# Gate logits as a 97th FFN column, the last 96 FFN columns unpacked, and VectorE steps split in halves, in a planned attention + SwiGLU kernel

## The chip, the cores and the metric

The kernel runs on one core of one Trainium2 chip. The metric is device microseconds of one execution; a kernel's time is the median of its runs.

## The reference

One activation x of 2048 tokens by 512 features (bf16) goes through two branches, which a gate mixes per token:

```python
g = sigmoid((x * gate_w).sum(-1, keepdims=True))
# branch a: 32 heads of 16, causal sliding window of 256 tokens
qkv = (x @ wqkv)                      # 512 -> 3 * 512
scores = q @ k.T * 16 ** -0.5         # kept where 0 <= query - key < 256
a = softmax(scores) @ v @ wo
# branch b: SwiGLU with F = 1376
b = (silu(x @ w1) * (x @ w3)) @ w2
out = g * a + (1 - g) * b
```

## The kernel before

**Tiling.** Tokens are cut into four tiles t of 512 (and sixteen m of 128). Heads come in four groups c of eight. F = 1376 is ten chunks f of 128 columns and a last one of 96 (`NFC` = 11, `FL` = 96). x stands transposed in SBUF (`xT`), the first half by TensorE transposes, the second by DMA transposes.

**Attention.** `add_proj` computes Q and K of one (c, t): four matmuls of 128 x 512 into one PSUM bank, then a copy to SBUF. K is copied twice, once with the odd and once with the even heads set to zero, by the factors in `maskEO`; `evac_k` (L336) does this in one VectorE instruction of 1024 elements per partition. A *burst* (`add_burst`, L636) computes the scores of up to 512 query columns for four head pairs, into the four banks of the PSUM tile `big`; ScalarE takes one exponential over them (L644); GpSimd cuts the window's edges (L660), and for some edges VectorE does (L654). There are 76 bursts, 4 or 5 for each (c, t). `add_pv` (L710) multiplies by V and by ones (for the denominators) into two banks; `turn` (L720) transposes each bank into SBUF, `norm` (L729, L730) divides both halves in two instructions, `back` (L735) transposes into `OT`, and `add_out` (L589, L596) multiplies by wo, mixes and stores.

**FFN.** `add_up` (L460) computes w1 and w3 of one (t, f) into a bank each. With silu(v) = v/2 (1 + tanh(v/2)), ScalarE takes the tanh (L436), VectorE multiplies twice (L441, L468) into `hT`. The last 96 columns are handled by `add_up_last` for two token tiles at once: they are cut into pieces of 32 columns, four pieces stand side by side in the array's columns, and three units of 16 small matmuls (L510) take the place of four units of four. `add_down` (L559) multiplies by w2 in 11 matmuls, and the result is scaled by (1 - g)/2 from `omg` (L565 on ScalarE, L568 on VectorE).

**Gate.** gate_w is broadcast to 128 partitions early by a GpSimd DMA (L163). `add_z` (L403): 16 VectorE multiplies with a running sum give the logits `zt`. The first half reads the x tiles that the transposes used, the second half a copy of x loaded anew, 1 MB, into a part of `OT` that is still free (L166). `add_gate`: a small tanh (L414) and two small VectorE steps (L417, L419) give `gq` and `omg`.

**What sets the order.** Everything after the first loads is an `Op` with its engine, an assumed duration, what it depends on, and which buffers it takes and frees: four PSUM banks `g`, the tile `big`, nine exponential buffers and others. A planner places ops by assumed times, one by one, and writes each engine's instruction order, which the engines then follow with semaphores. Bursts have due times 2.66 us apart. Where a burst isn't due, other work fills TensorE: projections, V, FFN units in a fixed sequence. Two rules matter here. While at most one bank is free (`tight`), ScalarE and VectorE prefer work that frees a bank; this rule stands in both kernels. And a first matmul of an FFN pair (`o.gate`) steps back while a tanh waits on ScalarE:

```python
elif o.kind == "ffn":
    k = 2 if backlog < 1 or not o.gate else 3.5
```

Of the kernel before, what the change touches and what calls it, by code (L numbers as in the profile page):

```python
# [22 lines left out]
def kernel(  # L23
# [37 lines left out]
    w1_sb = pp.tile([P, NDC, F], BF16, name="w1_sb")  # L61
# [4 lines left out]
    maskEO = pp.tile([P, 1, 2, 1], F32, name="maskEO")  # L66
    scr = pp.tile([P, 2], F32, name="scr")
    zt = pp.tile([P, NT], F32, name="zt")
# [3 lines left out]
    smpool = ctx.enter_context(tc.tile_pool(name="sm", bufs=3))  # L72
    ps = ctx.enter_context(tc.tile_pool(name="ps", bufs=1, space=bass.MemoryType.PSUM))

    class Op:
        def __init__(self, engs, dur, fn, deps=(), acq=(), rel=(), rank=0.0, need=None, kind="", lag=0.0):
            self.engs = engs if isinstance(engs, tuple) else (engs,)
            self.dur, self.fn, self.rank, self.kind, self.lag = dur, fn, rank, kind, lag
            self.deps = [d for d in deps if d is not None]
            self.acq, self.rel, self.need = acq, rel, need  # L80
            self.start = self.end = self.eng = None
            self.users = []
            self.gate = False
            self.cont, self.head, self.tiled = False, self, False
            ops.append(self)
# [21 lines left out]
    def x_dma(t, h):  # L107
        if t == 0:
            xs = xp.tile([P, 2, D], BF16, name=f"xs{h}")[:]
        else:  # L110
            if h == 0:
                xs_tiles["pair"] = xp.tile([P, 4, D], BF16, name="xs23")
            xs = xs_tiles["pair"][:, 2 * h:2 * h + 2, :]
        nc.sync.dma_start(
            out=xs,
            in_=x2d[512 * t + 256 * h:512 * t + 256 * (h + 1), :].rearrange("(m p) d -> p m d", p=P))
        xs_tiles[2 * t + h] = xs
# [41 lines left out]
    gw = OT[:, S:S + D]  # L159
    xn = OT[:, 2 * S:4 * S].rearrange("p (m d) -> p m d", d=D)  # L160

    def gate_dma():
        nc.gpsimd.dma_start(out=gw, in_=gate_w.rearrange("(x d) -> x d", x=1).to_broadcast([P, D]))  # L163

    def xn_dma():
        nc.sync.dma_start(out=xn, in_=x2d[S // 2:S, :].rearrange("(m p) d -> p m d", p=P))  # L166
# [7 lines left out]
    land["wo"], land["xn"], land["gate"] = 40.0, 40.0, 10.0  # L174
# [9 lines left out]
    nc.vector.tensor_reduce(out=maskEO[:, 0, 0, :], in_=eo[:], axis=mybir.AxisListType.X, op=ALU.add)  # L184
    nc.vector.tensor_scalar(out=maskEO[:, 0, 1, :], in0=maskEO[:, 0, 0, :], scalar1=-1.0, scalar2=1.0,
# [14 lines left out]
    gate_dma()  # L200
# [100 lines left out]
    def add_proj(c, t0, t1, is_q):  # L301
# [4 lines left out]
        hold("g", key, 1)  # L306
# [25 lines left out]
        def evac_k(eng):  # L332
            kt = qk_tile[(c, t)][0][:, 2 * o0:2 * (o0 + n)].rearrange("p (j i b) -> p j i b", i=2, b=HK)
            src = g_tile[key][:, 0:n].rearrange("p (j x b) -> p j x b", x=1, b=HK)
            sh = [P, n // HK, 2, HK]
            nc.vector.tensor_tensor(out=kt, in0=src.to_broadcast(sh), in1=maskEO[:].to_broadcast(sh),  # L336
                                    op=ALU.mult)
# [12 lines left out]
        else:  # L350
            bs = [Op("DVE", 1.16 * n / 512 + 0.05, evac_k, [a], rel=[("g", key)], rank=-0.5)]
# [45 lines left out]
    z_op, gate_op = [], {}  # L397

    def add_z(m):

        def f(eng):
            x = xs_tiles[m // 2][:, m % 2, :] if m < NT // 2 else xn[:, m - NT // 2, :]
            nc.vector.scalar_tensor_tensor(out=x, in0=x, scalar=1.0, in1=gw, op0=ALU.mult,  # L403
                                           op1=ALU.mult, accum_out=zt[:, m:m + 1])

        deps = xT_op[m // 2] if m < NT // 2 else [loads["xn"]]
        z_op.append(Op("DVE", 0.7, f, deps + [loads["gate"]], rank=1.5))

    def add_gate(t):

        ms = slice(4 * t, 4 * t + 4)

        def th(eng):
            nc.scalar.activation(out=zt[:, ms], in_=zt[:, ms], func=ACT.Tanh, scale=0.5)  # L414

        def fin(eng):
            nc.vector.tensor_scalar(out=gq[:, ms], in0=zt[:, ms], scalar1=0.5,  # L417
                                    scalar2=0.5, op0=ALU.mult, op1=ALU.add)
            nc.vector.tensor_scalar(out=omg[:, ms], in0=zt[:, ms], scalar1=-0.25,  # L419
                                    scalar2=0.25, op0=ALU.mult, op1=ALU.add)  # L420

        d = Op("ACT", 0.25, th, z_op[4 * t:4 * t + 4], rank=1.0)
        gate_op[t] = Op("DVE", 0.35, fin, [d], rank=1.0)
# [3 lines left out]
    def h_of(t):  # L427
        if t not in h_tile:
            h_tile[t] = sb.tile([P, NFC, 512], BF16, name=f"hT{slot('hT', t)}")
        return h_tile[t]  # L430

    def half_swish(tl, key, kt_, kh, m):

        def th(eng):
            tl["tt"] = sb.tile([P, 512], BF16, name=f"tt{slot('tt', kt_)}")
            nc.scalar.activation(out=tl["tt"][0:m, :], in_=g_tile[key][0:m, :], func=ACT.Tanh,  # L436
                                 scale=0.5)

        def s1(eng):
            tl["h1"] = sb.tile([P, 512], BF16, name=f"h1_{slot('h1', kh)}")  # L440
            nc.vector.scalar_tensor_tensor(out=tl["h1"][0:m, :], in0=tl["tt"][0:m, :], scalar=1.0,  # L441
                                           in1=g_tile[key][0:m, :], op0=ALU.add, op1=ALU.mult)
        return th, s1

    first_h = {}

    def add_up(t, f):

        kg, ku, kt_, kh = ("G", t, f), ("U", t, f), ("tt", t, f), ("h1", t, f)
# [3 lines left out]
        hold("h1", kh, 1)  # L453
        tl = {}

        def pe(key, wsb, d0):
            def fn():
                b = bank(key) if d0 == 0 else g_tile[key]
                for dc in range(d0, d0 + 1):
                    nc.tensor.matmul(b[:], lhsT=wsb[:, dc, f * P:(f + 1) * P],  # L460
# [4 lines left out]
        th, s1 = half_swish(tl, kg, kt_, kh, P)  # L465

        def s2(eng):
            nc.vector.tensor_tensor(out=h_of(t)[:, f, :], in0=tl["h1"][:], in1=g_tile[ku][:],  # L468
                                    op=ALU.mult)
# [3 lines left out]
        a0, a = pe_unit(0.87, [pe(kg, w1_sb, i) for i in range(NDC)], [w], acq=[("g", kg)],  # L473
# [3 lines left out]
        b = Op("ACT", 0.6, th, [a], rel=[("g", kg)], acq=[("tt", kt_)], rank=0.3, kind="tanh")  # L477
        a0.gate = True
        d = Op("DVE", 0.68, s1, [b], rel=[("g", kg), ("tt", kt_)], acq=[("h1", kh)])
        new = t not in first_h  # L480
        if new:
            hold("hT", t, 4)
        e = Op("DVE", 0.68, s2, [d, u] + ([] if new else [first_h[t]]),
               rel=[("g", ku), ("h1", kh)], acq=[("hT", t)] if new else [])
        first_h.setdefault(t, e)
        up_done.setdefault(t, []).append(e)
        return [a0, u0]

    def add_up_last(ta, tb):

        f0 = (NFC - 1) * P
        keys = [("L", ta, i) for i in range(3)]
        kt_, kh = [("tt", ta, "L", i) for i in range(2)], [("h1", ta, "L", i) for i in range(2)]
        for k, n in zip(keys, (2, 2, 3)):
            hold("g", k, n)
        for i in range(2):
            hold("tt", kt_[i], 1)
            hold("h1", kh[i], 2 - i)  # L500
        tiles = [[(w1_sb, 0, ta), (w1_sb, 1, ta), (w1_sb, 2, ta), (w1_sb, 2, tb)],
                 [(w3_sb, 0, ta), (w3_sb, 1, ta), (w3_sb, 2, ta), (w3_sb, 2, tb)],
                 [(w1_sb, 0, tb), (w1_sb, 1, tb), (w3_sb, 0, tb), (w3_sb, 1, tb)]]
        assert FL == 96

        def pe(i, dc):
            def fn():
                b = bank(keys[i]) if dc == 0 else g_tile[keys[i]]
                for u, (w, p, t) in enumerate(tiles[i]):
                    nc.tensor.matmul(b[32 * u:32 * u + 32, :],  # L510
                                     lhsT=w[:, dc, f0 + 32 * p:f0 + 32 * p + 32],
                                     rhs=xT[:, dc, 512 * t:512 * (t + 1)],
                                     start=(dc == 0), stop=(dc == NDC - 1), skip_group_check=True)
            return fn

        def prod(eng, t, lo, hi, h1, key, h0, u0):
            n = hi - lo
            nc.vector.tensor_tensor(out=h_of(t)[lo:hi, NFC - 1, :], in0=h1["h1"][h0:h0 + n, :],
                                    in1=g_tile[key][u0:u0 + n, :], op=ALU.mult)

        x = [a + b for a, b in zip(xdep(512 * ta, 512 * ta + 512), xdep(512 * tb, 512 * tb + 512))]
        units = [pe_unit(0.9, [pe(i, dc) for dc in range(NDC)], [loads["wb"]], acq=[("g", keys[i])],
                         kind="ffn", more=x) for i in range(3)]
        for a0, _ in units:
            a0.tiled = True
        tls = [{}, {}]
        sw = [half_swish(tls[0], keys[0], kt_[0], kh[0], P),
              half_swish(tls[1], keys[2], kt_[1], kh[1], 64)]
# [468 lines left out]
```

## Time and profile before

| | us |
|---|---|
| median of 3 runs | 234.25 (234.06 to 234.43) |
| the profiled execution | 234.06 |
| its span, first to last instruction | 232.3 |
| TensorE busy | 222.7 |
| VectorE, ScalarE, GpSimd busy | 181.1, 176.6, 173.7 |
| start of the first and of the last burst | 12.9, 213.2 |

Times inside the profile count from the span's start. DVE is VectorE, ACT ScalarE, POOL GpSimd, SP the engine that issues most DMAs, PE TensorE's matmuls and PEld its weight loads, which overlap them. Busy shares are means over the span; where an engine waited, the profile names what ended the wait.

### The profile page before, as it was taken

To read this page: it belongs to the slowest core of one execution; us is meant where nothing else is said; L and a number is where in the kernel's file an instruction comes from. 1 tells how busy PE (TensorE), PEld (TensorE's weight loads), DVE (VectorE), ACT (ScalarE), POOL (GpSimd) and SP (SyncE) were. 2 spreads that over 40 slices of the span, in tenths; PEclk is the share of its full clock that TensorE was granted. 3 is DMA by queue.
4 is the path that set the end of the run, shared out by engine and by line. 5 is a ranking of instruction groups with operands and counts; after the bars stand their busy time and mean duration, and the time that the engine had idled before them with its cause. 6 is when DMAs were issued, how large, how long until landed. Compare 5 with 4: busy or idle time off the path is not lost.

```text
span 232.3 us, 7327 instructions
## 1 busy us (share of the span) xinstructions
PE 222.7 (96%) x3073; PEld 102.7 (44%) x3107; DVE 181.1 (78%) x321; ACT 176.6 (76%) x147; POOL 173.7 (75%) x395
## 2 busy tenths in 40 slices
PE   7999999999999999999999999999999999999992
PEld 3644344435344444435353535444444444454441
DVE  1698798999999895977867894959887977867544
ACT  2589987789887889787988898878788876877220
POOL 8059888899989888868778877778687867767500
PEclk9999999999999999999999999999999999999999
DMA  6999990020200000000000000000000020100202
GB/s 170 342 268 306 293 367 15 3 48 3 51 2 3 3 0 3 4 1 3 0 3 3 3 0 3 0 3 4 0 3 4 0 95 3 69 24 23 70 3 90
DMA packets 16096, 13.27 MB, mean 57 GB/s; under 512 B 6080, under 2 KB 15776, under 8 KB 16064
## 3 DMA queue, kind: packets, MB, share of 16 engines
q1 hardware_dynamic: 15104, 11.44, 16.6%
q0 software_dynamic: 432, 1.25, 2.5%
q8 instruction: 24, 0.39, 0.7%
q10 hardware_dynamic: 528, 0.13, 0.3%
q14 instruction: 8, 0.07, 0.1%
HBM read 8.55 MB, written 2.10 MB: 46 GB/s over the span
## 4 chain that ended last, share of the span: by engine, by line
PE 85%; ACT 4%; POOL 4%; issue 4%; DVE 1%; DMA 1%; DVEq 0%; POOLq 0%; ACTq 0%
PE big L636 10%; PE g_4000 L559 1%; PE g_4322 L559 1%; PE g_2777 L559 1%; PE g_2299 L559 1%; PE g_1951 L559 1%; POOL e_3211 L660 1%; POOL e_3063 L660 1%; PE g_4162 L559 1%; PE g_2058 L559 1%; PE g_4507 L559 1%; PE g_4482 L559 1%; PE g_4520 L559 1%; PE g_1328 L559 1%; PE g_2549 L559 1%
## 5 line engine op out<-in xcount | busy, mean ns | idle before, releaser
L460 PEld LDWEIGHTS <-w_sb 128*128 128x128 bf16 x320 | 28.8, 98 | 35.7 <-issue 4.7
L710 PEld LDWEIGHTS <-Vn 64*32 64x32 bf16 x736 | 15.5, 91 | 4.3 <-issue 2.3
L710 PEld LDWEIGHTS <-Vs 64*32 64x32 bf16 x736 | 15.5, 91 | 0.1
L735 DVE STREAM_TRANSPOSE OT<-on 128x512 bf16<-128x512 bf16 (+1 forms) x17 | 11.4, 671 | 0.1
L589 PEld LDWEIGHTS <-OT 128*128 128x128 bf16 x68 | 6.3, 98 | 6.9 <-issue 0.4
L321 PEld LDWEIGHTS <-wq_sb 128*128 128x128 bf16 x68 | 6.3, 98 | 6.7 <-issue 0.6
L321 PEld LDWEIGHTS <-wk_sb 128*128 128x128 bf16 x68 | 6.1, 98 | 6.5 <-issue 1.0
L368 PEld LDWEIGHTS <-xT 128*128 128x128 bf16 x64 | 5.7, 98 | 6.6 <-issue 0.4
L392 POOL DMA_DIRECT2D Vs<-Vn x4 | 2.5, 617 | 7.2 <-ACT Vn L376 7.2
L559 PEld LDWEIGHTS <-hT_3267 128*128 128x128 bf16 (+1 forms) x44 | 4.1, 97 | 4.9
L559 PEld LDWEIGHTS <-hT_1265 128*128 128x128 bf16 (+1 forms) x44 | 4.0, 98 | 4.8 <-issue 0.6
L559 PEld LDWEIGHTS <-hT_383 128*128 128x128 bf16 (+1 forms) x44 | 4.0, 98 | 4.6 <-issue 0.2
L403 DVE SCALAR_TENSOR_TENSOR OT<-OT 128x512 bf16<-128x512 bf16 x8 | 6.0, 762 | 0.0
L559 PEld LDWEIGHTS <-hT_2312 128*128 128x128 bf16 (+1 forms) x44 | 3.9, 98 | 4.7 <-issue 0.4
L660 POOL TENSOR_SCALAR_AFFINE_SELECT e_4456<-e_4456 64x256 bf16<-64x256 bf16 x8 | 3.5, 432 | 1.8 <-ACT e_4456 L644 1.4
L720 DVE STREAM_TRANSPOSE xs_4595<-g_4527 128x256 f32<-128x256 f32 x1 | 0.5, 450 | 5.2 <-PE g_4528 L710 5.2
L958 PE MATMUL g_141<-tt_87 128*128 128x512 bf16 x7 | 3.2, 630 | 1.3 <-DVE tt_87 L104 1.3
L660 POOL TENSOR_SCALAR_AFFINE_SELECT e_269<-e_269 64x256 bf16<-64x256 bf16 x6 | 3.7, 611 | 0.8 <-ACT e_269 L644 0.6
L660 POOL TENSOR_SCALAR_AFFINE_SELECT e_967<-e_967 64x256 bf16<-64x256 bf16 x6 | 3.8, 639 | 0.4
L660 POOL TENSOR_SCALAR_AFFINE_SELECT e_686<-e_686 64x256 bf16<-64x256 bf16 x6 | 3.2, 532 | 0.9 <-ACT e_686 L644 0.6
L660 POOL TENSOR_SCALAR_AFFINE_SELECT e_4280<-e_4280 64x256 bf16<-64x256 bf16 x6 | 2.8, 469 | 1.1 <-ACT e_4280 L644 0.8
L510 PEld LDWEIGHTS <-w_sb 128*32 128x32 bf16 x96 | 2.2, 96 | 2.9 <-issue 1.1
(949 smaller groups left out, 849.5 us busy)
## 6 DMA issues: line engine op xcount, KB each, us to landing
out_dram<-ot SPq DMA_DIRECT2D x15, 128.0 KB, 1.7
w_sb<-in_B_w_dram SPq DMA_DIRECT2D x2, 864.0 KB, 7.4
w_sb<-in_B_w_dram SPq DMA_DIRECT2D x1, 1280.0 KB, 7.6
Vs<-Vn POOLq DMA_DIRECT2D x8, 136.0 KB, 4.1
w_sb<-in_B_w_dram SPq DMA_DIRECT2D x2, 512.0 KB, 8.7
OT<-in_A_x_dram SPq DMA_DIRECT2D x1, 1024.0 KB, 10.4
e_89<-in_A_wqkv_dram SPq DMA_DIRECT2D x1, 512.0 KB, 5.7
xs_98<-in_A_x_dram SPq DMA_DIRECT2D x2, 256.0 KB, 5.9
```

What stands on the lines that cost most here:

```text
L321: nc.tensor.matmul(b[:, 0:n], lhsT=(wq_sb if is_q else wk_sb)[:, dc, c * P:(c + 1) * P], rhs=xT[:, dc, t0:t1], start=(dc == 0), stop=(dc = ...
L368: nc.tensor.matmul(b[:], lhsT=xT[:, c, m * P:(m + 1) * P], rhs=wv_sb[:, c, :], start=(c == 0), stop=(c == NDC - 1))
L392: nc.gpsimd.dma_start(out=Vs[0:HK, ms, 0:VW], in_=Vn[HK:P, ms, 0:VW])
L403: nc.vector.scalar_tensor_tensor(out=x, in0=x, scalar=1.0, in1=gw, op0=ALU.mult, op1=ALU.mult, accum_out=zt[:, m:m + 1])
L460: nc.tensor.matmul(b[:], lhsT=wsb[:, dc, f * P:(f + 1) * P], rhs=xT[:, dc, t * 512:(t + 1) * 512], start=(dc == 0), stop=(dc == NDC - 1))
L559: nc.tensor.matmul(b[:], lhsT=h_tile[t][0:fs, f, (m % 4) * P:(m % 4 + 1) * P], rhs=w2_sb[0:fs, f, :], start=(f == 0), stop=(f == NFC - 1))
L589: nc.tensor.matmul(b[:, 0:n], lhsT=OT[:, c * S + m * P:c * S + (m + 1) * P], rhs=wo_t[c // 2][:, c % 2, n0:n1], start=(c == 0), stop=(c == ...
L636: nc.tensor.matmul(big[:, u, col:col + q1 - q0], lhsT=kt[32 * u:32 * u + 32, (j % 8) * P:(j % 8 + 1) * P], rhs=qt[32 * u:32 * u + 32, q0 - ...
L660: nc.gpsimd.affine_select(out=tri, in_=tri, pattern=[[0, 4], [-1 if far else 1, HK]], compare_op=ALU.is_ge, fill=0.0, base=-1 if far else ...
L710: nc.tensor.matmul(pv[i][32 * u:32 * u + 32, a - qa:b - qa], lhsT=v_of(j, i, 4 * c + u), rhs=e_tile[k][i * HK:i * HK + HK, u, col:col + b ...
L735: nc.vector.transpose(out=OT[:, c * S + qa:c * S + qb], in_=st["on"][:, 0:nb].rearrange("p b i d -> p (b i d)"))
L958: nc.tensor.matmul(b[:], lhsT=warm[:, 0:P], rhs=warm[:], start=(i == 0), stop=(i == NWARM - 1))
```

## The change

- The last 96 columns of F are a chunk like the others, per token tile: four matmuls for w1 and four for w3. `add_up_last` and its packed matmuls go.
- The gate's logit is a 97th column: `w1_sb` has one column more, loaded with gate_w by a GpSimd DMA of 512 two-byte elements, issued when the eighth burst is recorded. The tanh of this chunk covers 97 rows (into float32, tile `xs2`), and its row 96 is tanh of half the logit. SP sends that row to a DRAM tile `zd` and fetches it back as 128 x 4 (`put`, `get`); two VectorE steps then make `gq` and `omg`. The 16 VectorE sums, the second load of x, the broadcast and the small tanh go.
- The last chunk stands fifth in a tile's sequence of chunks (ninth in the first tile).
- K's copy becomes two VectorE instructions of 512 elements; `norm` becomes two pairs, one for each half, which may start after the first transpose.
- The planner's rule on waiting tanhs goes. The bookkeeping that the packing needed (`first_h`, `tiled`) goes with it.

The diff, cut to its core:

```diff
-    w1_sb = pp.tile([P, NDC, F], BF16, name="w1_sb")
+    w1_sb = pp.tile([P, NDC, F + 1], BF16, name="w1_sb")
...
     def gate_dma():
-        nc.gpsimd.dma_start(out=gw, in_=gate_w.rearrange("(x d) -> x d", x=1).to_broadcast([P, D]))
-
-    def xn_dma():
-        nc.sync.dma_start(out=xn, in_=x2d[S // 2:S, :].rearrange("(m p) d -> p m d", p=P))
+        nc.gpsimd.dma_start(out=w1_sb[:, :, F:F + 1],
+                            in_=gate_w.rearrange("(c p x) -> p c x", p=P, x=1))
...
-        def evac_k(eng):
-            kt = qk_tile[(c, t)][0][:, 2 * o0:2 * (o0 + n)].rearrange("p (j i b) -> p j i b", i=2, b=HK)
-            src = g_tile[key][:, 0:n].rearrange("p (j x b) -> p j x b", x=1, b=HK)
-            sh = [P, n // HK, 2, HK]
-            nc.vector.tensor_tensor(out=kt, in0=src.to_broadcast(sh), in1=maskEO[:].to_broadcast(sh),
-                                    op=ALU.mult)
+        def evac_k(i):
+            def f(eng):
+                kt = qk_tile[(c, t)][0][:, 2 * o0:2 * (o0 + n)].rearrange(
+                    "p (j i b) -> p j i b", i=2, b=HK)[:, :, i, :]
+                src = g_tile[key][:, 0:n].rearrange("p (j b) -> p j b", b=HK)
...
+                    nc.vector.tensor_scalar_mul(out=kt, in0=src, scalar1=maskEO[:, i:i + 1])
+            return f
...
-            bs = [Op("DVE", 1.16 * n / 512 + 0.05, evac_k, [a], rel=[("g", key)], rank=-0.5)]
+            bs = [Op("DVE", d, evac_k(i), [a], rel=[("g", key)], rank=-0.5) for i in range(2)]
...
-    def add_z(m):
...
-    def add_gate(t):
...
+    def add_gate(t, b, tl, row):
...
+        def put(eng):
+            nc.sync.dma_start(out=zd[t:t + 1, :], in_=tl["tt"][row:row + 1, :])
+
+        def get(eng):
+            st["gt"] = smpool.tile([P, 4], F32, name="gt")
+            nc.sync.dma_start(out=st["gt"][:], in_=zd[t, :].rearrange("(j p) -> p j", p=P))
...
+        d = Op("SP", 3.5, put, [b])
+        e = Op("SP", 4.5, get, [d])
+        gate_op[t] = Op("DVE", 0.35, fin, [e])
...
     def add_up(t, f):
+        fs = fsz(f)
+        has_z = f == NFC - 1
...
+            m = fs + 1 if has_z and key == kg else fs
...
-                    nc.tensor.matmul(b[:], lhsT=wsb[:, dc, f * P:(f + 1) * P],
+                    nc.tensor.matmul(b[0:m, :], lhsT=wsb[:, dc, f * P:f * P + m],
                                      rhs=xT[:, dc, t * 512:(t + 1) * 512],
...
+            if has_z:
+                tl["tt"] = xp.tile([P, 512], F32, name="xs2")
+                m = fs + 1
...
-        a0.gate = True
...
-    def add_up_last(ta, tb):
...
-        def norm(eng):
-            rden = sb.tile([P, 2, 16, 1], F32, name="rden")
...
+        def norm(i):
+            def f(eng):
...
-        n1 = Op("DVE", 0.5 + nq * 0.0011, norm, [b0, b1], rank=rk)
+        n0 = Op("DVE", 0.4 + nq * 0.0007, norm(0), [b0], rank=rk)
+        n1 = Op("DVE", 0.4 + nq * 0.0007, norm(1), [b1, n0], rank=rk)
...
-        for f in range(NFC - 1):
+        zat = 4 if t else 8
+        for n, f in enumerate(list(range(zat)) + [NFC - 1] + list(range(zat, NFC - 1))):
...
-            if t % 2 == 0 and f == 10:
-                ffn += held + add_up_last(t, t + 1)
-                held = []
...
-        if t % 2 == 0 and 10 > 9:
-            ffn += add_up_last(t, t + 1)
...
-                        k = 2 if backlog < 1 or not o.gate else 3.5
+                        k = 2
...
-            if not wo_t and o in burst_ops[7:] and done.issuperset(z_op[0:4]):
+            if o is burst_ops[7]:
                 wo_dma()
-                xn_dma()
-            done.add(o)
+                gate_dma()
```

## The prediction

> **What bounds the kernel now.** I read the page's engine table first, then its slices, then the stretches, the chain of waits and the wait list.
>
> ```profile
> span 232.3 us, 7327 instructions
> ...
> PE 222.7 (96%) x3073; PEld 102.7 (44%) x3107; DVE 181.1 (78%) x321; ACT 176.6 (76%) x147; POOL 173.7 (75%) x395
> ...
> PE   7999999999999999999999999999999999999992
> ...
> PEclk9999999999999999999999999999999999999999
> ```
>
> TensorE is busy 96% of the span, in every slice but the first and the last, at a granted clock of 0.998. The others stand at 75 to 78%. A busy TensorE need not be at its peak, so I check that it does not wait. The stretches cut at the first and the last score burst:
>
> ```profile
> 0.00:12.90 12.90, 11.40 (x72) 6.56 (x73) 6.19 (x17) 5.60 (x10) 5.53 (x19) 1.00 0.86 269
> 12.90:213.20 200.30, 196.76 (x2801) 88.50 (x2835) 165.42 (x286) 167.10 (x134) 163.81 (x367) 1.00 0.16 44
> 213.20:232.30 19.10, 14.53 (x206) 7.63 (x207) 9.49 (x20) 3.94 (x4) 4.38 (x10) 0.98 0.17 57
> ```
>
> The columns after the length are PE, PEld, DVE, ACT and POOL. In the 200.3 us between the bursts TensorE lacks 3.54 us in all. The chain of waits says the same ("PE 85%", the rest in pieces), and the wait list says for what TensorE waited:
>
> ```profile
> PEld L636 <- DVE e_899 L654: 0.4, 1, 0.4
> PEld L710 <- DVE h_1_1326 L441: 0.4, 1, 0.4
> PEld L710 <- DVE hT_3267 L468: 0.4, 1, 0.4
> ...
> PEld L710 <- DVE hT_383 L468: 0.2, 1, 0.2
> ```
>
> With two of 0.2 us on the matmuls themselves (e_1713 L654, hT_2312 L468) that is 1.8 us behind VectorE, and nothing behind ScalarE or GpSimd. The rest is called issue: short gaps at changes of matmul shape. So the time is the sum of TensorE's instructions plus a start of 4.6 us and an end of about 4 us. A change counts if it lengthens that sum or makes TensorE wait.
>
> **TensorE, the term that counts.** Removed are six packed units (L510), three for each pair of token tiles. The chain prices the first three, beside a full-width unit:
>
> ```profile
> 49.36 0.86 PE g_934 L460 x4
> ...
> 60.16 0.98 PE g_1179 L510 x16
> 61.13 0.43 PE g_1199 L510 x8
> ...
> 61.89 0.55 PE g_1199 L510 x8
> 62.44 0.86 PE g_1235 L510 x16
> ```
>
> 0.98 + 0.43 + 0.55 + 0.86 = 2.82 us, and 5.64 for both triples. Added are eight full-width units (w1 and w3 for each of four tiles), at 0.86 us 6.88. The 97th weight column is free: matmuls over fewer than 128 columns or rows (the 96-row ones of L559, 0.38 us) last as long as the others. Difference **+1.24 us**. Lower bound: the second triple, by the starts in the timeline (152.16 to 153.81, 155.39 to 156.39, 156.70 to 157.03), took 2.98; 5.80 for both, or 5.96 if both cost that, so +0.92. Upper bound: had the packed groups cost exactly a quarter each, they would be 6 x 0.86 = 5.16, so +1.72. I take 1.24, from the chain.
>
> The Trainium skill (TensorEngine Tiling (Array Packing), Theoretical Speedup and Key Properties) gives a factor of up to four for at most 32 weight columns, and says that a change of tiling mode drains the array. The rows agree with the second: 0.98 against 0.86 for a packed unit that follows a full-width one. By the factor alone the sum would be 1.72 and the time 0.5 us higher.
>
> Everything else on TensorE keeps count and size. In the changed kernel's instruction order, 76 bursts stand as before; every stretch between two bursts without attention output holds at least ten full-width matmuls, eight after the four narrow bursts, as in the old order (which has packed ones among them). With a burst every 2.60 us in both kinds of stretch and an exponential of 1.88 us, a written order with a hole over 0.2 us would show a stretch with one matmul fewer. There is none, so the new order leaves TensorE no hole, if the other queues keep up.
>
> **VectorE.** Removed: 16 gate sums (L403), 11.37 us with their accumulator reads; two product steps, 46 to 44, 1.4 us. Added: each K copy (L336) in two halves. A half has 512 elements per partition from PSUM; the nearest row is Q's copy (L330), 0.68 us. 15 x (2 x 0.68 - 1.22) = 2.1; two small ones at 0.42 a half, 0.3. Normalization in halves: by the rows of the 256-wide case, 0.25 + 0.42 a half, 15 x (2 x 0.67 - 0.34 - 0.75) = 3.8. Sum: -11.4 - 1.4 + 2.4 + 3.8 = -6.6 us, 181 to about 174. It lies beside TensorE and costs nothing, since VectorE has slack; if the cover were gone, K's longer hold on its bank (1.36 against 1.22) would show as 0.1 us at each of 17 projections. ScalarE loses four small activations (0.83 us), nothing on the path.
>
> **Transfers.** Removed: the 1 MB reload of x (26.47 to 36.87 us) and the early gate broadcast on GpSimd (0.69 us of queue). No one on TensorE waited for either: zero. Added on SP, four times: one row of 2 KB out to DRAM and 512 single elements back. SP has nothing else queued then, but on VectorE the gate's two small steps wait for the return, and behind them stand the transposes that free attention output's banks. Their price is bounded by these rows (KB, us to landing):
>
> ```profile
> Vs<-Vn POOLq DMA_DIRECT2D x8, 136.0 KB, 4.1
> ...
> wk_sb<-in_A_wqkv_dram ACTq DMA_DIRECT2D x1, 128.0 KB, 3.5
> ...
> OT<-in_gate_w_dram POOLq DMA_DIRECT2D x1, 128.0 KB, 6.6
> ...
> out_dram<-ot SPq DMA_DIRECT2D x2, 64.0 KB, 1.5
> ```
>
> Out: 1.5 us. Back: between 1.5 and 6.6; I take 3.5, the row that also has 512 short pieces. A round trip is 3.0 to 8.1, likely 5.0 us. The room: for the last tile the tanh stands behind the 59th exponential, done 3.0 us after its burst (0.54 + 1.88 + 0.6), and the gate step behind K's copy in the stretch after the 62nd burst, 2.5 us after that burst. With 2.60, 2.60 and 2.10 us between those bursts the room is 7.3 - 3.0 + 2.5 = 6.8 us; the third tile has about 7.3, the others more. Likely cost zero; at the upper bound 1.3 and 0.8 us, 2.1 in all.
>
> Once, GpSimd loads the gate as a column, 512 elements of two bytes, behind the second Vs pair. In the new order that pair stands after two masks of the sixth exponential (done at 28.6 us), so the load goes out near 31 and, by 4.1 to 6.6 us, lands at 35.1 to 37.6 (38.1 with half a microsecond of delay). The 97-column matmul stands a unit and a burst after the tenth burst's start: 36.98 + 0.33 + 0.22 + 0.86 = 38.4. Zero, but closely; a load twice as slow costs up to 6 us. Neither price goes below nothing: TensorE waits for no gate transfer now.
>
> The Trainium skill (DMA: Bandwidth & Descriptors, Rules for kernel authors) says that a strided last dimension lowers to one descriptor per element, which speaks against both of these transfers. No row here shows elements that small; its fixed cost of about 2.0 us a DMA would make the round trip an estimated 4 us and the sum the same.
>
> **Sum.** The profiled execution took 234.06 us, 1.76 more than its span. 234.06 + 1.24 = 235.30. The median of the runs is 0.19 higher, 234.25, so I forecast **235.5 us**, +0.5%. A measurement of this kernel can tell about 0.2% (0.47 us) from no change.
>
> **Rivals.**
> 1. *New waits on top of the sum.* The old planner held back a first FFN matmul while a tanh was waiting; this falls away, so a bank may be taken early and freed late, and the gate adds the two waits above. For it: four banks only, and the bounds of 2.1 us (round trip) and 6 us (column). Against: the full stretches in the new order, and rows near the durations that the planner assumes. Price: 1 to 3.5 us more, 236.5 to 239.
> 2. *Not slower: relief of VectorE and GpSimd.* VectorE loses 6.6 us, most between 11 and 70 us, where it is fullest (19.7 of 20 us from 40 to 60), and there the masks on GpSimd are slowest (611 and 639 ns against 410 later). If this freed TensorE's 1.8 us of waits, the time would be 234.25 + 1.24 - 1.8 = 233.7. It decides from 0.77 us (no measurable change) and from 1.71 us (faster). Against: only 1.0 of the 1.8 us lies before 70 us (e_899, hT_383, h_1_1326), which would leave 0.24 us slower, and VectorE's work grows later.
> 3. *The packed work is cheaper to lose than it seems*, if its mode changes cost the neighbours too: the lower bound, 235.2; in the forecast's range.
>
> **How the numbers follow.** The sum alone, 234.9 to 236.2 (0.92 and 1.72 us, with some tenths of order on top): 0.72. Rival 1: 0.16. Rival 2: 0.12, of which 0.08 within 0.2% and 0.04 faster. Slower by over 0.2%: 0.72 + 0.16 = 0.88. The range leaves out rival 2 (0.12) and about half of rival 1 (0.08): 234.8 to 237.3.
>
> **What would show it.** Right: TensorE's busy time up by 1 to 1.5 us, its gap between the bursts still near 3.5 us, the last burst some 0.4 us later and the end 1.2 us later (the order has 4 matmuls more after the last burst), VectorE near 174 us. Wrong: a wait of TensorE on the gate column near 38 us, VectorE waiting for the DRAM return with TensorE idle behind it, or bursts more than 2.60 us apart because banks are held. If TensorE's missing time falls below 2 us, rival 2 is at work.

## The result and the profile after

| | before | after |
|---|---|---|
| median, us | 234.34 (234.06 to 234.59, 4 runs) | 235.80 (235.64 to 236.05, 4 runs) |
| ratio to before | | 1.0063, interval [1.0046, 1.0081] |
| profiled execution, its span | 234.06, 232.3 | 235.75, 234.1 |
| granted clock | 0.998 | 0.998 |
| start of the last burst | 213.16 | 213.56 |
| start of the last VectorE step (`ot`) | 229.01 | 230.26 |

The changed kernel is slower by 0.63%, 1.46 us between the medians; 235.5 was forecast. The page's first line, engine line and line of the chain of waits:

```profile
span 234.1 us, 7214 instructions
...
PE 223.0 (95%) x3008; PEld 103.6 (44%) x3043; DVE 177.0 (76%) x337; ACT 176.1 (75%) x144; POOL 168.3 (72%) x395
...
PE 92%; DMA 3%; issue 2%; DVE 1%; SPq 0%; DVEq 0%
```

The others have become emptier (VectorE 181.1 to 177.0, GpSimd 173.7 to 168.3), and the end is later all the same: the chain runs over TensorE for 92% of the span. The stretches, cut where the prediction cut them (PE, PEld, DVE, ACT, POOL after the length):

```profile
12.90:213.20 200.30, 196.32 (x2728) 89.72 (x2759) 160.97 (x299) 165.97 (x130) 158.91 (x367) 1.00 0.16 38
213.20:234.10 20.90, 15.65 (x210) 8.07 (x211) 11.51 (x25) 4.11 (x5) 4.52 (x11) 0.98 0.16 52
```

Between the bursts TensorE seems to lack 3.98 us, 3.54 before. The wait list gives what it waited for there:

```profile
PEld L564 <- DVE e_893 L582: 0.4, 1, 0.4
PEld L564 <- DVE h_0_661 L451: 0.4, 1, 0.4
PEld L638 <- DVE Vn L371: 0.4, 1, 0.4
PEld L638 <- DVE bsb L496: 0.2, 1, 0.2
PEld L638 <- DVE hT_1263 L457: 0.4, 1, 0.4
PEld L638 <- DVE h_0_1510 L451: 0.2, 1, 0.2
```

That is 2.0 us of idle time of weight loads with VectorE named as what ended it (1.8 before, two of those on matmuls), and none of it names the gate or its column. Kernel 4 will show that no such line is a wait of TensorE's matmuls. The timeline shows the column's matmul, the last tile's gate transfers and the end:

```profile
12.98 0.40 PE L564 MATMUL big<-qt_175,kt_174 32*128 32x320 bf16 x8
...
30.99 0.78 POOL L155 DMA_DIRECT2D w_sb<-in_gate_w_dram  x1
...
38.45 1.03 PE L434 MATMUL g_689<-xT,w_sb 128*97 128x512 bf16 x4
...
172.23 0.24 SPq L396 DMA_DIRECT2D zd<-xs_3506  x1
173.45 0.37 SPq L400 DMA_DIRECT2D gt<-zd  x1
179.23 0.37 DVE L404 TENSOR_SCALAR gq<-gt 128x4 f32<-128x4 f32 x1
...
228.93 0.38 PE L517 MATMUL g_4635<-xs_580,OT 128*128 128x256 bf16 x2
...
230.26 0.48 DVE L524 SCALAR_TENSOR_TENSOR ot<-g_4635,gq,bsb 128x256 bf16<-128x256 f32 x1 [0.44 <-DMA out_dram<-ot]
```

No wait stands in brackets behind the 97-column matmul or the gate step. The last `ot` step starts 1.25 us later than before:

```profile
229.01 0.48 DVE L596 SCALAR_TENSOR_TENSOR ot<-g_4637,gq,bsb 128x256 bf16<-128x256 f32 x1 [0.45 <-DMA out_dram<-ot]
```

**A measure for the experiments.** The first burst starts between 12.67 and 13.90 us in the profiled executions, as the first loads land. So besides the medians I use the *stretch*: from the start of the first burst to the end of the last `ot` step. Before it is 229.49 - 12.94 = 216.55 us, after 230.74 - 12.98 = 217.76: **+1.21**. It comes from one profiled execution of each kernel; three orders of the changed kernel's matmuls (the change, kernels 2 and 9) agree on it within 0.01.

### The profile page after: what moved, and what is told of

Read it like the earlier page. It is cut to its first block, busy times and chain, and to the rows that moved or that the text cites. A ratio compares the mean times of both kernels' runs of the same rounds, so it can differ in the third digit from the quotient of the medians.

```text
span 234.1 us, 7214 instructions
## 1 busy us (share of the span) xinstructions
PE 223.0 (95%) x3008; PEld 103.6 (44%) x3043; DVE 177.0 (76%) x337; ACT 176.1 (75%) x144; POOL 168.3 (72%) x395
## 3 DMA queue, kind: packets, MB, share of 16 engines
q0 software_dynamic: 416, 1.12, 2.2%
## 4 chain that ended last, share of the span: by engine, by line
PE 92%; DMA 3%; issue 2%; DVE 1%; SPq 0%; DVEq 0%
PE big L564 11%; DMA wq_sb<-in_A_wqkv_dram 2%; PE g_1391 L487 1%; PE g_4312 L487 1%; PE g_3536 L487 1%; PE g_3048 L487 1%; PE g_2285 L487 1%; PE g_1620 L487 1%; PE g_4101 L487 1%; PE g_2556 L487 1%; PE g_4500 L487 1%; PE g_4515 L487 1%; PE g_2038 L487 1%; PE g_2773 L487 1%; PE g_1761 L487 1%
## 5 line engine op out<-in xcount | busy, mean ns | idle before, releaser
L434 PEld LDWEIGHTS <-w_sb 128*128 128x128 bf16 (+2 forms) x352 | 32.5, 100 | 38.0 <-issue 3.9
L588 POOL TENSOR_SCALAR_AFFINE_SELECT e_4440<-e_4440 64x256 bf16<-64x256 bf16 x8 | 3.3, 410 | 1.8 <-ACT e_4440 L572 1.5
L493 ACT ACTIVATE bsb<-g_4500,omg 128x512 bf16<-128x512 f32 x1 | 0.7, 687 | 5.1 <-PE g_4500 L487 5.1
L329 DVE TENSOR_SCALAR kt_250<-g_252,maskEO 128x512 bf16<-128x512 f32 x2 | 1.4, 746 | 2.8 <-PE g_252 L310 2.8
L588 POOL TENSOR_SCALAR_AFFINE_SELECT e_4254<-e_4254 64x256 bf16<-64x256 bf16 x6 | 2.7, 452 | 1.1 <-ACT e_4254 L572 0.8
L588 POOL TENSOR_SCALAR_AFFINE_SELECT e_1394<-e_1394 64x256 bf16<-64x256 bf16 x6 | 2.5, 422 | 1.3 <-ACT e_1394 L572 1.0
L588 POOL TENSOR_SCALAR_AFFINE_SELECT e_416<-e_416 64x256 bf16<-64x256 bf16 x6 | 2.5, 410 | 1.3 <-ACT e_416 L572 1.0
L588 POOL TENSOR_SCALAR_AFFINE_SELECT e_1753<-e_1753 64x256 bf16<-64x256 bf16 x6 | 2.5, 410 | 1.2 <-ACT e_1753 L572 0.9
L588 POOL TENSOR_SCALAR_AFFINE_SELECT e_3486<-e_3486 64x256 bf16<-64x256 bf16 x6 | 2.6, 436 | 1.0 <-ACT e_3486 L572 0.7
```

What stands on the lines that cost most here:

```text
L329: nc.vector.tensor_scalar_mul(out=kt, in0=src, scalar1=maskEO[:, i:i + 1])
L434: nc.tensor.matmul(b[0:m, :], lhsT=wsb[:, dc, f * P:f * P + m], rhs=xT[:, dc, t * 512:(t + 1) * 512], start=(dc == 0), stop=(dc == NDC - 1))
L588: nc.gpsimd.affine_select(out=tri, in_=tri, pattern=[[0, 4], [-1 if far else 1, HK]], compare_op=ALU.is_ge, fill=0.0, base=-1 if far else ...
```

## The experiments

My theory: only the unpacked matmuls count (+1.24), all else is covered. The rivals: the new waits, relief through a freer VectorE, and a smaller price of the packing. All results in one table: "time" is the median minus that of the kernel before, measured beside it (234.34 to 234.56 us), with the ratio's interval beside it; "stretch" is the difference to 216.55 us.

| kernel | time | ratio, interval | stretch |
|---|---|---|---|
| the change | +1.46 | 1.0063 [1.0046, 1.0081] | +1.21 |
| 1 before, only unpacked | +3.43 | 1.016 [1.0132, 1.0189] | +3.12 |
| 2 after, whole K copy and norm | +1.59 | 1.007 [1.0051, 1.0088] | +1.21 |
| 3 before, no tanh rule | +0.42 | 1.0023 [0.9999, 1.0048] | +0.47 |
| 4 before, five `ot` buffers | -0.62 | 0.9976 [0.9962, 0.999] | -0.66 |
| 5 after, one unit twice | +4.33 | 1.018 [1.0133, 1.0226] | +4.14 |
| 6 after, column two bursts later | +3.17 | 1.0134 [1.008, 1.0189] | +3.31 |
| 7 unpacked, no gate sums | +1.22 | 1.0043 [1.002, 1.0066] | +1.28 |
| 8 packed, no gate sums | +0.24 | 1.0016 [1.0001, 1.0031] | +0.20 |
| 9 after, tanh rule back | +1.53 | 1.0062 [1.0042, 1.0083] | +1.21 |
| 10 as 1, last chunk last | +2.04 | 1.0081 [1.0066, 1.0096] | +2.09 |
| 11 after, long gate return | +4.11 | 1.0169 [1.0156, 1.0183] | +4.14 |
| 12 as 1, sums with one operand | +1.12 | 1.0056 [1.0039, 1.0072] | +1.48 |

### 1. The packing alone

```diff
-            if t % 2 == 0 and f == 10:
-                ffn += held + add_up_last(t, t + 1)
...
+        zat = 4 if t else 8
+        for n, f in enumerate(list(range(zat)) + [NFC - 1] + list(range(zat, NFC - 1))):
```

> The kernel before, with the packing alone undone: eight full-width units of the last 96 columns take the place of the six packed ones, at the places where the changed kernel has them; the gate stays on VectorE, K's copy and the normalization stay whole, the rule on waiting tanhs stays. Theory (the time is TensorE's sum): 8 x 0.86 - 5.64 = +1.24 us, 235.5 to 235.6, ratio 1.005, the whole of the change. Rival 1 (new waits make part of the change's 1.46 us): clearly less, +0.3 to +0.8, because the gate's transfers, the halves and the missing rule are not in it.

Measured +3.43, not the sum's +1.24. The timeline of this kernel shows one place that the change does not have: VectorE runs gate sums (L403) one behind the other, GpSimd's masks crawl, and TensorE's attention output (L711) waits for one.

```profile
52.77 6.59 POOL L661 TENSOR_SCALAR_AFFINE_SELECT e<-e 64x256 bf16<-64x256 bf16 x8
...
53.24 2.84 POOL L661 TENSOR_SCALAR_AFFINE_SELECT e<-e 64x256 bf16<-64x256 bf16 x1
...
53.29 0.68 DVE L403 SCALAR_TENSOR_TENSOR OT<-OT 128x512 bf16<-128x512 bf16 x1
...
55.13 0.68 DVE L403 SCALAR_TENSOR_TENSOR OT<-OT 128x512 bf16<-128x512 bf16 x1
...
55.74 0.68 DVE L378 CAST Vn<-g 128x512 bf16<-128x512 f32 x1
...
57.54 0.29 PE L711 MATMUL g<-e,Vs 64*32 64x256 bf16 x4 [1.01 <-POOL e L661]
58.02 0.30 PE L711 MATMUL g<-e,Vn 64*32 64x256 bf16 x8 [0.19 <-POOL e L661]
```

Eight masks took 6.59 us, where eight of 0.41 make 3.3. One of them took 2.84: it began at 53.24, just ahead of four sums that followed each other from 53.29, and ended at 56.08, just after VectorE had gone over to a copy out of PSUM at 55.74. The two waits of TensorE shown make 1.2 us; the surplus over +1.24 is 1.9, and some 0.7 of it has no line of its own. Two explanations were left: the sums lock the masks out, or VectorE is merely too full there. Kernels 7, 8, 10 and 12 part them.

### 7 and 8. Without the gate sums

Kernel 7 is kernel 1, and kernel 8 the kernel before, each without the sums, the broadcast and the second load of x; the logits are zero.

```diff
+    nc.vector.memset(zt[:], 0.0)
...
-    gate_dma()
...
-    for m in range(NT):
-        add_z(m)
...
-                xn_dma()
```

> The kernel before with the packing undone, as in the first experiment, and also without the gate's 16 VectorE sums, the broadcast and the second load of x (the gate's logits are left at zero). The first experiment took 3.4 to 3.7 us instead of 1.24. Theory 2 (in the unpacked order the sums are not covered: through VectorE and the masks that GpSimd makes beside it, they hold up attention output): the surplus goes, 235.6 to 235.8, ratio 1.005. Rival (the surplus is an accident of where the planner put the unpacked units): stays near 238, ratio 1.012 to 1.016.

> The kernel before, with the packing, but without the gate's 16 VectorE sums, the broadcast and the second load of x (the gate's logits are left at zero). The prediction booked their loss at zero. If that holds: 234.5 within 0.3 us. If the sums cost something in the packed order as well, it is faster by what they cost, at most the 1.8 us that TensorE waited behind VectorE.

Unpacked, the sums' removal is worth 3.12 - 1.28 = 1.84 us of stretch, and what is left is the price of the packing. In the same stretch of time fourteen masks now take as long as eight did:

```profile
52.88 6.56 POOL L661 TENSOR_SCALAR_AFFINE_SELECT e<-e 64x256 bf16<-64x256 bf16 x14
```

Packed, it is worth nothing (+0.20). In the kernel before, sums stood back to back in the same place (53.62 to 55.93), but took turns with the masks: two of the three sums lasted 0.88 us instead of 0.68, and no mask over 0.93.

```profile
53.91 4.13 POOL L660 TENSOR_SCALAR_AFFINE_SELECT e_967<-e_967 64x256 bf16<-64x256 bf16 x6
...
55.12 0.88 DVE L403 SCALAR_TENSOR_TENSOR OT<-OT 128x512 bf16<-128x512 bf16 x1
```

### 10. The last chunk in another place

```diff
-        for n, f in enumerate(list(range(zat)) + [NFC - 1] + list(range(zat, NFC - 1))):
+        for n, f in enumerate(range(NFC)):
```

> The kernel before with only the packing undone, as in the first experiment, and the last chunk moved to another place (last) in each tile's sequence of chunks; the gate's sums stay on VectorE. Theory (the sums on VectorE slow the masks of GpSimd and nothing covers that once the packed groups are gone): over 2 us above the kernel before, 236.5 to 238. Rival (the first experiment's surplus was an accident of the one place where sums and masks met): only the packing's price is left, 235.6 to 236.

+2.04, between the two forecasts: some 0.9 us of stretch over the packing's price instead of 1.9. The wait on a mask is gone (longest mask 0.93 us); in the same place TensorE now waits 0.34 us for V's copy, which had queued behind the sums on VectorE:

```profile
54.80 0.88 DVE L403 SCALAR_TENSOR_TENSOR OT<-OT 128x512 bf16<-128x512 bf16 x1
...
55.61 0.68 DVE L378 CAST Vn<-g 128x512 bf16<-128x512 f32 x1
...
56.34 0.59 PE L368 MATMUL g<-e,xT 128*128 128x512 bf16 x2 [0.34 <-DVE Vn L378]
```

So the surplus depends on where sums and masks meet. About 0.5 us of this kernel's surplus is not assigned to a line.

### 12. Sums that read one operand

```diff
-            nc.vector.scalar_tensor_tensor(out=x, in0=x, scalar=1.0, in1=gw, op0=ALU.mult,
-                                           op1=ALU.mult, accum_out=zt[:, m:m + 1])
+            nc.vector.tensor_reduce(out=zt[:, m:m + 1], in_=x, axis=mybir.AxisListType.X, op=ALU.add)
```

> The first experiment's kernel (only the packing undone) with each of the 16 gate sums replaced by a VectorE sum over x alone, which reads one operand where the multiply-and-sum read two; the product with gate_w is left out, the order of every engine is the same. Theory A (VectorE instructions with two SBUF operands lock GpSimd's masks out, for as long as they follow each other): the longest mask falls from 2.84 us to below 1, TensorE's wait of 1.0 us on a mask goes, and from the first burst to the end it takes 217.8 to 218.7 us where the first experiment took 219.67; about 236.3 us. Theory B (VectorE is merely too full there, whatever its instructions read): as the first experiment, 219.4 to 219.9 and about 238 us.

The order and the sums' duration stay as in kernel 1 (0.68 us; 0.59 from one to the next, 0.61 there), the second operand goes, and with it the surplus: 218.03 us of stretch against 219.67. The timeline has four sums in a row as before:

```profile
52.08 2.46 DVE L403 TENSOR_REDUCE zt<-OT 128x1 f32<-128x512 bf16 x4
```

The summary of the masks' line (minimum, median and maximum in ns, then the first and the last start):

```profile
L660 POOL TENSOR_SCALAR_AFFINE_SELECT e<-e x368: 407/412/929, 15.1 to 218.4; 64x256 bf16<-64x256 bf16 x184
```

No mask takes over 0.93 us, and TensorE waits for none. That VectorE was merely too full is ruled out: it was as full here. (The accumulator reads, 0.08 us each, went with the old form.)

Kernel 12 drops more than an operand: the sum no longer writes 128 x 512 values back, and no accumulator runs along. The trace of the kernel before parts these. All 15 masks that ran wholly within a step of L441 (the same kind of instruction with a result of the same size, but one operand from PSUM) took 0.41 us. Beside the norm's product (L730, two operands from SBUF, no accumulator) a mask that began 0.04 us after the product's start took 0.93. So what holds the masks goes with two operands from SBUF.

### 2. K's copy and the norm whole

Kernel 2 is the changed kernel with `evac_k` and `norm` as in the kernel before.

```diff
...
-            bs = [Op("DVE", d, evac_k(i), [a], rel=[("g", key)], rank=-0.5) for i in range(2)]
+            bs = [Op("DVE", 1.16 * n / 512 + 0.05, evac_k, [a], rel=[("g", key)], rank=-0.5)]
...
-        n0 = Op("DVE", 0.4 + nq * 0.0007, norm(0), [b0], rank=rk)
-        n1 = Op("DVE", 0.4 + nq * 0.0007, norm(1), [b1, n0], rank=rk)
+        n1 = Op("DVE", 0.5 + nq * 0.0011, norm, [b0, b1], rank=rk)
```

> The changed kernel with K's copy in one VectorE instruction and the normalization in one pair, as before. Theory: VectorE's added time is covered, so no difference from the changed kernel: 235.8, ratio to before 1.005 to 1.007. Rival 1 (K's bank and attention output's banks held longer): 0.3 us or more faster than the changed kernel, 235.5 or less.

The stretch is that of the change, 217.76 us, though VectorE works 170.1 us instead of 177.0. The halves cost VectorE 6.9 us and the kernel nothing.

### 3 and 9. The planner's rule

Kernel 3 is the kernel before without the rule on waiting tanhs, kernel 9 the changed kernel with it. Kernel 3's edit, which kernel 9 takes back:

```diff
-                        k = 2 if backlog < 1 or not o.gate else 3.5
+                        k = 2
```

> The kernel before without the planner's rule that a first FFN matmul steps back while a tanh waits. Theory: the order changes but TensorE's sum does not, 234.3 within 0.3 us, ratio 0.999 to 1.001. Rival 1: banks are taken early and freed late, TensorE waits, 1 us or more slower.

> The changed kernel with one rule of the planner taken back: tanh, evacuations and bank-freeing VectorE work no longer go ahead of exponentials when few PSUM banks are spare. Theory (the rule decides little, TensorE has full matmuls to hand either way): the changed kernel's time, 235.8 us within 0.4. Rival (the rule costs something by itself, as the kernel before without its own tanh rule hints at the opposite by +0.4): over 0.5 us away to either side.

(What was recorded for kernel 9 describes the other rule, `tight`, which stands in both kernels. Its edit puts back the rule on waiting tanhs and nothing else.)

In the new order the rule changes nothing (217.76 with it and without). In the old one its loss may cost 0.4 us; the interval just includes no change, and I leave that open.

### 5. One unit twice

The w3 unit of the last chunk is computed twice in each tile, four full-width units more.

```diff
-        u0, u = pe_unit(0.87, [pe(ku, w3_sb, i) for i in range(NDC)], [w], acq=[("g", ku)],
+        twice = 2 if has_z else 1
+        u0, u = pe_unit(0.87 * twice, [pe(ku, w3_sb, i) for i in range(NDC)] * twice, [w], acq=[("g", ku)],
...
```

> The changed kernel with the w3 unit of each tile's last chunk computed twice into the same bank (the second time overwrites the first). It adds four full-width units of 0.86 us to TensorE and nothing else. Theory (the time is TensorE's sum): 4 x 0.86 = +3.45 us over the changed kernel, 239.2, ratio 1.021. Rival: TensorE has holes that take some of it, +2 us or less.

Over the change +2.87 by the table's times (4.33 - 1.46) and +2.93 by the stretches, where four units of 0.86 are 3.44. TensorE's last matmuls and the last `ot` steps show where the rest went:

```profile
232.49 1.04 PE L518 MATMUL g<-xs,OT 128*128 128x256 bf16 x8
...
233.41 0.88 DVE L525 SCALAR_TENSOR_TENSOR ot<-g,gq,bsb 128x256 bf16<-128x256 f32 x2 [2.29 <-ACT bsb L494]
```

From the first burst (13.60 us) to the end of TensorE's last matmul it is 219.93 us, in the change 229.31 - 12.98 = 216.33. So TensorE's end moves by 3.60 us: the added matmuls are paid in full. Behind it the last `ot` steps take 0.76 us where the change takes 1.43, since they no longer wait for a store. That gives 0.67 back, and 3.60 - 0.67 = 2.93. TensorE is the bound.

### 6. The gate column later

```diff
+LATE = 9
...
+            if o is burst_ops[LATE]:
```

> The changed kernel with the gate column's load issued two bursts later in the written order, behind the masks of the eighth exponential. By the changed kernel's trace it would be issued near 36.9 us and land near 41.4, while the 97-column matmul stands ready at 38.45. Theory (TensorE has no slack later, so an early stall is found at the end): TensorE waits about 2.9 us there and the time is 2.5 to 3 us over the changed kernel, 238.5. Rival: later slack takes it back, under 1 us.

The load went out at 36.75 instead of 30.99 us and landed 3.4 us later. The timeline of TensorE:

```profile
40.20 1.07 PE L435 MATMUL g<-xT,w_sb 128*97 128x512 bf16 x4 [1.89 <-DMA w_sb<-in_gate_w_dram]
```

A wait of 1.89 us on TensorE moves the stretch's end by 2.10: it is paid in full, and less than the 2.5 to 3 us expected. I had taken the transfer at 4.5 us, hence the larger wait expected.

### 11. A longer way for the gate

```diff
+HOPS = 3
...
+            row = zd[t:t + 1, :]
+            for i in range(HOPS):
+                nxt = dr.tile([1, 512], F32, name=f"hop{t}_{i}")
+                nc.sync.dma_start(out=nxt[0:1, :], in_=row)
+                row = nxt[0:1, :]
...
```

> The changed kernel with three more hops between the gate's writing to DRAM and its reading back, of which the planner knows nothing, so that the round trip is some 9 us where it was 3.3. Theory (the trip has 7.0 to 9.9 us of room at the four tiles and costs nothing at 3.3): the gate is late by 0 to 2.3 us at the tiles, VectorE waits for it and the end moves by 0.5 to 3 us. Rival (VectorE has slack behind the gate step, so that even a late gate costs nothing): 235.8 within 0.3.

The trip took 9.6 us at the last tile (174.3 to 183.85). VectorE's waits of the four tiles in the timeline, and TensorE's at the last two:

```profile
50.77 0.34 DVE L410 TENSOR_SCALAR gq<-gt 128x4 f32<-128x4 f32 x1 [0.44 <-DMA gt<-hop]
...
86.58 0.17 DVE L410 TENSOR_SCALAR gq<-gt 128x4 f32<-128x4 f32 x1 [2.15 <-DMA gt<-hop]
...
135.10 0.28 DVE L410 TENSOR_SCALAR gq<-gt 128x4 f32<-128x4 f32 x1 [2.70 <-DMA gt<-hop]
...
136.11 2.32 PE L440 MATMUL g<-xT,w_sb 128*128 128x512 bf16 x10 [1.04 <-DVE t L654]
...
183.85 0.17 DVE L410 TENSOR_SCALAR gq<-gt 128x4 f32<-128x4 f32 x1 [2.52 <-DMA gt<-hop]
...
184.76 0.38 PE L440 MATMUL g<-xT,w_sb 128*128 128x512 bf16 x1 [0.89 <-DVE t L654]
```

VectorE stands for 7.8 us; of 2.70 and 2.52 us TensorE feels 1.04 and 0.89, by the way that the prediction named (the transposes behind the gate step keep the banks). The stretch is 2.93 us longer than the change's; TensorE's gaps make 2.3 of that, the rest I have not found. So rival 1's mechanism exists; at 3.3 us the trip is far from it.

### 4. More buffers at the end

Both kernels wait some 0.45 us in the last `ot` step for a store, since `ot` has three buffers.

```diff
-    smpool = ctx.enter_context(tc.tile_pool(name="sm", bufs=3))
+    smpool = ctx.enter_context(tc.tile_pool(name="sm", bufs=5))
```

> The kernel before with five instead of three buffers for the stored output tile. In the trace the last VectorE step waited 0.45 us for a store to leave its buffer. Theory (the end after TensorE's last matmul is a chain through that wait): 0.45 us faster, 233.9, ratio 0.998. Rival: the stores themselves set the end, so it stays at 234.3.

The last steps now follow each other without that wait, and this version is faster than both kernels, by 0.24% [0.1, 0.38] against the one before. The last four take 2.40 us where the kernel before takes 3.08 (226.41 to 229.49). These 0.68 us are the gain: the wait of 0.45, and 0.2 by which the steps now follow each other more closely.

```profile
227.34 2.40 DVE L596 SCALAR_TENSOR_TENSOR ot<-g,gq,bsb 128x512 bf16<-128x512 f32 x4 [0.17 <-PE g L589]
```

## Why the prediction held, and where its steps did not

**The sum of TensorE's matmuls: right.** +1.24 forecast; +1.21 and +1.28 of stretch in the change and in kernel 7. The last burst came 0.40 us later (0.4 forecast), the last VectorE step 1.25 (1.24). From the first burst to the end of TensorE's last matmul it is 228.05 - 12.94 = 215.11 us before and 229.31 - 12.98 = 216.33 after, +1.22. The prediction had nothing for the end of the span: behind the last packet of the last store another 2.1 us pass, 1.6 before, with no work left. In the change's trace an 8 KB packet of a queue for instructions ends together with the span, at 234.05; that the end waited for it is not shown. So the profiled execution rose by 1.69 us, the median by 1.46, 0.3 over the forecast of 235.5. Rival 3, the smaller price of +0.92, is not what the stretches show.

**TensorE's missing 3.5 us: wrong.** The prediction read 3.54 us between the bursts as short gaps and waits. The page of before shows 3073 matmuls and 3107 weight loads: records of matmuls are missing, and they leave gaps of 0.05 to 0.16 us, which the wait list calls issue where they are long enough. Kernel 4 has the same matmuls with all records. The engine line of its page:

```profile
PE 226.0 (97%) x3107; PEld 102.1 (44%) x3107; DVE 180.9 (78%) x321; ACT 176.6 (76%) x147; POOL 174.2 (75%) x395
```

And the stretch from its first to its last burst:

```profile
13.85:214.09 200.24, 200.21 (x2828) 88.45 (x2828) 165.35 (x286) 167.08 (x134) 164.23 (x367) 1.00 0.17 42
```

TensorE is busy for 200.21 of 200.24 us there, and of the 15 gaps of 0.16 us that the wait list of before has on matmuls as issue none is left. (The ends of matmuls are modelled: one of 512 columns is drawn 0.38 us long, while in a row they follow 0.22 us apart, so a wait under 0.16 would not show. A longer one does in a complete trace, as the 1.01 us in kernel 1.)

The 1.8 us behind VectorE were no waits either. Kernel 4's wait list still has such lines on weight loads, of the same 0.4 us that stand 72 times ahead of score matmuls with nothing to wait for, while TensorE shows no gap:

```profile
PEld L636 <- issue: 30.5, 72, 0.4
...
PEld L636 <- DVE e L654: 0.4, 1, 0.4
```

A weight load overlaps the matmuls, so its idle time is not TensorE's. "Busy time up by 1 to 1.5 us" failed for the missing records as well: +0.26 in two traces that lack 34 and 35 records, and "still near 3.5 us" compared nothing but those. Complete traces of the new matmuls show the rise, the page of kernel 9 for one:

```profile
PE 227.5 (97%) x3043; PEld 103.8 (44%) x3043; DVE 179.1 (76%) x339; ACT 175.9 (75%) x142; POOL 168.3 (72%) x395
```

227.5 - 226.0 = 1.5, and 227.3 in kernel 2 makes 1.3. This is a rough measure: kernel 3, with the matmuls of the kernel before in another order, has 226.9. (The sign given for rival 2, missing time below 2 us, would have been seen in kernel 4, which frees VectorE of nothing.)

**Rival 2, relief through VectorE: the price was not there.** It would have freed 1.8 us of waits, which were none; kernel 8 relieves VectorE by 8.9 us (172.2) in the old order and gains nothing, kernel 2 by 6.9 in the new.

**VectorE's load: mis-sized.** 174 forecast, 177.0 measured. K's halves added 3.1 us (L329 22.66 against L336 19.55), 2.4 forecast; the norm's 5.6 (7.92 + 15.41 against 5.66 + 12.11), 3.8 forecast. It costs nothing (kernel 2).

**The gate's sums: right here, wrong as a rule.** That their loss brings nothing holds in the packed order (kernel 8). But unpacking alone costs 3.4 us (kernel 1); the change stays at 1.2 because it takes the sums away at the same time. The prediction priced its parts one by one and saw no link between them. It had seen slow masks where VectorE is fullest (rival 2) and put them down to nothing in particular.

**Transfers: right, with room.** Round trip 3.2 to 3.35 us (5.0 forecast, 3.0 to 8.1 as bounds); 173.45 + 2.1 - 172.23 = 3.3 at the last tile, where the gate step came 7.0 us after the issue (6.8 forecast). The column was issued at 30.99 us (31 forecast), landed after 4.5, at 35.48, for a matmul at 38.45 (38.4 forecast). Kernels 6 and 11 show that both waits exist: data that come late hold TensorE, and the end moved by 2.10 and 2.93 us.

## What to carry to other kernels

Where one engine has no gap at all, its instructions are the bill: price what is added there and check that the rest arrives in time. Before gaps of a tenth or two are read as waits, compare the count of matmuls with that of weight loads; and idle time of weight loads is no wait of the matmuls that they overlap. And price the parts of a change together: a VectorE instruction that reads two SBUF operands costs nothing while nobody waits for GpSimd, and 1.8 us after another part has moved the place where the two meet.

## What the runs showed of the hardware

- A GpSimd mask (64 x 256, usually 0.41 us) that starts just ahead of a row of two-operand VectorE instructions can be held for the whole row: 2.84 us in kernel 1. With one-operand sums of the same length the longest took 0.93.
- It works both ways. In the kernel before, a product with two SBUF operands (L730) that began 0.08 us after a mask lasted 0.87 us instead of 0.69, and the mask its usual 0.41; a mask that began 0.04 us after such a product lasted 0.93, and the product its 0.69.
- The Trainium skill (SBUF — State Buffer, section SBUF: two separate sides) says that VectorE instructions with two SBUF inputs and GpSimd instructions take a shared pair of ports as an exclusive lock, each for one whole instruction. Kernels 1 and 12 agree on the lock and on what triggers it. But the mask of 2.84 us was not let in between four such instructions, while in the kernel before the two took turns; what decides between these is open.
- Transfers of tiny elements were quicker than feared: 512 elements of two bytes landed 4.5 us (the change) and 3.4 us (kernel 6) after their issue on GpSimd, 512 of four bytes 2.1 to 2.2 us after theirs on SP (the change).
